# Attention, then two gated MLPs, on one core: PSUM as a ring of four slots, V's products in two bursts per head pair, softmax sums in another form

## The chip, the core and the metric

The kernel runs on one core of one Trainium2 chip. The metric is the device time of one execution in microseconds (us), from the runs of one chip; the version before has a median of 628.54 us over 3 runs (628.42 to 628.84).

## The reference, cut to what matters

```python
# batch 2, heads 8, seq 1152, head_dim 64
q_pool = q.reshape(B, H, S // 2, 2, D).mean(axis=3)           # 576 pooled queries a head
scores = scale * np.matmul(q_pool, k.transpose(0, 1, 3, 2))   # 576 x 1152
scores = scores - np.max(scores, axis=-1, keepdims=True)
attn = np.exp(scores)
attn = attn / (np.sum(attn, axis=-1, keepdims=True) + 1e-09)
x = np.matmul(attn, v)                                        # tokens 1152 x 512
h = x @ w_in;   g = h * np.tanh(softplus(h));   x = g @ w_out     # d_ff 2048
h = x @ w_in2;  g = np.where(h > 0, h, np.exp(h) - 1);  out = g @ w_out2
```

All tensors are float32. The weights of both MLPs come as 64-bit numbers and are turned into float32 on the chip.

## The kernel before, in words

The attention stage takes two heads at a time, a *pair*; there are 8 pairs. Scores are computed with the keys on the partitions: 9 key tiles of 128 keys (`kt`), and the 576 queries in two column groups, `c=0` with 256 and `c=1` with 320 columns. Each score tile (`qk`, line 364) is a sum of three products in a split of float32 into a high and a low part (`KH`/`KL`, `QH`/`QL`), and of a fourth one that adds the negative row maximum from `tops` by a product with `unit`. The two heads of a pair lie on the two halves of the partitions, so each product is two instructions on 64 rows that run side by side. ScalarE takes the exponential of the tile (`exp`, L373) into `pt`, for one key tile, or for two of group 0 at once.

Row maxima of the next pair are computed ahead of need (`peak_mm`, L284, L291, L298; `peak` on VectorE, L305 to L310), and are sent through DRAM into `tops` (`top_out`, `top_in`). V's products (`av`, L444) sum `vs` times `pt` over the 9 key tiles; they are plain float32, which the trace shows as two records for each matmul. The softmax sums come in two steps: `add` (L384) adds key tiles elementwise into two buffers, on GpSimd or VectorE as the table `who` says, and `total` (L399) multiplies by ones and so sums over the partitions. `spill`, `sum_out`, `sum_in`, `invert`, `inv_out` and `inv_in` carry the sums through DRAM and bring their reciprocals back as `rb`. `scale` (L461) multiplies V's product by it in PSUM, and `token_high` and `token_low` (L466, L471) write the two parts `XH` and `XL` for the MLPs.

PSUM has 8 banks, `banks`. Six of them are a ring of three slots of two banks, which `take()` gives out in turn to score tiles and maxima. Bank 6+c holds V's product of group c; the softmax sums and the last 128 columns of the maxima of the 64 left-over queries lie in the free columns of banks 6 and 7.

The order of the work is written out by tables. A step is one key tile, 18 steps a pair. `PLAN` (`FIRST` and `LAST` for the first and last pair) says at which step of a pair, or of the next one (steps over 17), an add, a product of V, a total and each link of the chain behind it are issued; `PREP` says the same for loads, splits and maxima of the next pair. Inside a step the lists go in the order pre, peak, the scores and their exponential, late, av, act, dve, rest, pool, sp. Every engine runs its own instructions in that order. The pieces of the first weights (`Weights`, L119 to L145) are converted in between, one per pair.

The MLP stage (`h_mm` L178, `out_mm` L744) follows. It uses the same 8 banks in another way, and starts with tokens of the first four pairs.

Of the kernel before, what the change touches and what calls it, by code (L numbers as in the profile page):

```python
# [22 lines left out]
def tile_pool_attention_mish_elu_mlp(  # L23
# [20 lines left out]
    P = 128  # L44
# [39 lines left out]
    class Weights:  # L84
# [98 lines left out]
    def attention():  # L183
        with ExitStack() as st:
            ap = st.enter_context(tc.tile_pool(name="attn", bufs=2))
            pools["f"] = st.enter_context(tc.tile_pool(name="f1", bufs=1))
            ring = cycle(range(3))
# [27 lines left out]
            raw_k, raw_q, kh, kl, qh, ql, vs = {}, {}, {}, {}, {}, {}, {}  # L215
            hops, tots, rbs, stat, neg, pts, adds, sc, sums_, acc, xs = {}, {}, {}, {}, {}, {}, {}, {}, {}, {}, {}
# [58 lines left out]
            def peak_mm(n, e):  # L275
# [19 lines left out]
                else:  # L295
                    side = banks[:, 6, 512 - P:]
# [3 lines left out]
            def peak(n, e):  # L300
# [5 lines left out]
                elif t > NQ:  # L306
                    nc.vector.tensor_reduce(m[:, :NQ, :, 2].rearrange("p t h -> p h t"), pt.rearrange("p h (t k) -> p h t k", k=P), axis=AX.X, op=ALU.max)
                else:
                    nc.vector.tensor_reduce(m[:, t, 0, 0:2], pt, axis=AX.X, op=ALU.max)
                    nc.vector.tensor_reduce(m[:, t, 0, 2:3], banks[:, 6, 512 - P:], axis=AX.X, op=ALU.max)  # L310
# [43 lines left out]
            def qk(n, c, kt, m, pt=None, part=slice(4)):  # L354
# [3 lines left out]
                terms = [(kh[n], qh[n]), (kl[n], qh[n]), (kh[n], ql[n]), (None, tops[n % 2])]  # L358
                sc[n, c, kt] = pt[:, :, :m * w].rearrange("p h (m w) -> p m h w", m=m)
                for t in range(m):  # L360
                    k0 = (kt + t) * P
                    for i, (x, y) in list(enumerate(terms))[part]:
                        for h in range(2):
                            nc.tensor.matmul(  # L364
                                pt[:, h, t * w:(t + 1) * w], x[half[h], k0:k0 + P] if x is not None else unit[half[h], :],
                                y[half[h], cols], start=(i == 0), stop=(i == len(terms) - 1),
                            )

# [7 lines left out]
            ADDS = {1: (0, 0, 1), 3: (1, 2, 3), 4: (0, None, 4), 5: (1, None, 5), 6: (0, None, 6), 7: (1, None, 7), 8: (0, None, 8)}  # L376

            def add(n, c, kt, eng):
                w = cut[c][1] - cut[c][0]
                if kt == 1:  # L380
                    adds[n, c] = ap.tile([P, 2, 2, 5 * D], F32, tag="add", name="add")
                x, i, j = ADDS[kt]
                d, p = adds[n, c][:, x, :, :w], pts[n, c]
                eng.tensor_tensor(d, d if i is None else p[:, i], p[:, j], op=ALU.add)  # L384

            def total(n, c):
                w = (cut[c][1] - cut[c][0]) // 2
# [69 lines left out]

            def scale(n, c):
                w = cut[c][1] - cut[c][0]
                x = xs[n, c] = acc.pop((n, c))[:, :w]  # L460
# [15 lines left out]
            def at(s, e, f, *args):  # L476
# [18 lines left out]
            PREP[2] = {
                "load_q": [-29, -29],
                "load_k": [-22, -20],
                "load_v": [-5, 2],
                "pool_q": -25,
                "high_q": -20,  # L500
                "high_k": [-21, -19],
                "blk_q": -18,
                "low_q": -12,
                "low_k": [-8, -15],
                "peak": [-30, -28, -26, -21, -15, -13, -8, -4, 0, 2],
                "top": [[3, 3], [0, 4]],
            }
            PLAN = {
                "who": [{1: 0, 3: 0, 4: 0, 5: 0, 6: 0, 7: 0, 8: 1}, {1: 0, 3: 0, 5: 1, 7: 0, 4: 0, 6: 0}],
                "add": [{1: 3, 3: 4, 4: 3, 5: 3, 6: 4, 7: 1, 8: 1}, {1: 1, 3: 1, 4: 4, 5: 3, 6: 3, 7: 2}],  # L510
                "av": [10, 10, 17, 17, 17, 17, 17, 17, 17, 22, 22, 22, 22, 26, 26, 26, 26, 28],
                "total": [13, 21],
                "chain": [[-1, 1, 1, 2, 5, 5, 9, 12, 13, 13], [-1, 1, 1, 3, 5, 6, 11, 13, 14, 17]],
                "two": [0, 2, 4, 7],
                "weight": [3, 6, 7, 10, 15, 16, 17, 5],
            }
            FIRST = {
                "who": [{1: 0, 3: 0, 4: 1, 5: 0, 6: 0, 7: 0, 8: 0}, {1: 0, 3: 1, 5: 1, 7: 0, 4: 0, 6: 0}],
                "add": [{1: 2, 3: 1, 4: 4, 5: 3, 6: 2, 7: 1, 8: 3}, {1: 2, 3: 2, 4: 4, 5: 1, 6: 3, 7: 1}],
                "av": [10, 10, 17, 17, 17, 17, 17, 17, 17, 22, 22, 22, 22, 26, 26, 26, 26, 28],  # L520
                "total": [13, 21],
# [368 lines left out]
```

## Time and profile before

| | |
|---|---|
| median of 3 runs | 628.54 us |
| span of the profiled execution, first to last instruction | 627.9 us |
| the runs' median less that span | 0.6 us |
| TensorE busy | 613.0 us, 98% of the span |
| VectorE, ScalarE, GpSimd busy | 447.2, 333.9, 224.2 us |
| attention stage, until the first matmul of L178 | 222.2 us |
| MLP stage | 405.7 us |

The profile is of one execution. Its span leaves out what lies before the first and after the last instruction. PE is TensorE, DVE VectorE, ACT ScalarE, POOL GpSimd, SP the engine that issues most DMAs. TensorE starts a matmul while the one before is still draining, so the records of neighbours overlap; how long a matmul holds the engine is read from the start of one record to the start of the next.

### The profile page before, as it was taken

To read this page: it belongs to the slowest core of one execution; us is meant where nothing else is said; L and a number is where in the kernel's file an instruction comes from. 1 tells how busy PE (TensorE), PEld (TensorE's weight loads), DVE (VectorE), ACT (ScalarE), POOL (GpSimd) and SP (SyncE) were. 2 spreads that over 40 slices of the span, in tenths; PEclk is the share of its full clock that TensorE was granted. 3 is DMA by queue.
4 is the path that set the end of the run, shared out by engine and by line. 5 is a ranking of instruction groups with operands and counts; after the bars stand their busy time and mean duration, and the time that the engine had idled before them with its cause. 6 is when DMAs were issued, how large, how long until landed. Compare 5 with 4: busy or idle time off the path is not lost.

```text
span 627.9 us, 11285 instructions
## 1 busy us (share of the span) xinstructions
PE 613.0 (98%) x4434; PEld 533.7 (85%) x4434; DVE 447.2 (71%) x694; ACT 333.9 (53%) x652; POOL 224.2 (36%) x210
## 2 busy tenths in 40 slices
PE   4899999999999999999999999999999999999997
PEld 3777677767766699999999999999999999999995
DVE  5897777878785566745647667669879788995453
ACT  3574665655654445443453454456657667664441
POOL 5688787887883212110113333332210101100000
PEclk9999999999999999999999999999999999999999
DMA  4424334253331444214223222322232223300011
GB/s 135 144 60 136 92 91 129 67 141 101 72 90 34 109 113 142 86 50 133 68 68 104 98 68 67 101 68 67 68 101 67 68 68 103 121 12 21 32 50 50
DMA packets 46975, 53.33 MB, mean 85 GB/s; under 512 B 13834, under 2 KB 36426, under 8 KB 46922
## 3 DMA queue, kind: packets, MB, share of 16 engines
q1 hardware_dynamic: 46698, 52.29, 28.4%
q8 instruction: 34, 0.56, 0.4%
q10 hardware_dynamic: 224, 0.33, 0.2%
q14 instruction: 19, 0.16, 0.1%
HBM read 50.14 MB, written 2.47 MB: 84 GB/s over the span
## 4 chain that ended last, share of the span: by engine, by line
PE 92%; DVE 3%; DMA 2%; SPq 1%; issue 1%; ACT 0%; DVEq 0%
PE banks L178 32%; PE banks L744 31%; PE banks L364 12%; PE banks L444 10%; PE banks L284 3%; PE banks L399 2%; DVE stat L305 2%; PE banks L298 1%; DMA rb<-pop 1%; DMA qr<-in_q_dram 1%; PE banks L291 0%; SPq L239 0%; DVE add L384 0%; DMA tot<-hop 0%; DVE part L769 0%
## 5 line engine op out<-in xcount | busy, mean ns | idle before, releaser
L123 POOL TENSOR_SCALAR wf<-wf 128x512 f32<-128x512 f32 x64 | 44.3, 693 | 252.7 <-ACT wf L119 222.2
L178 PE MATMUL banks<-XH,wh 128*128 128x384 f32 x384 | 129.5, 337 | 0.0
L178 PE MATMUL banks<-XL,wh 128*128 128x384 f32 x384 | 129.4, 337 | 0.0
L178 PE MATMUL banks<-XH,wl 128*128 128x384 f32 x384 | 129.4, 337 | 0.0
L373 ACT ACTIVATE pt<-banks 128x640 f32<-128x640 f32 (+2 forms) x113 | 87.3, 784 | 49.2 <-PE banks L364 30.4
L305 DVE TENSOR_REDUCE stat<-banks 128x2 f32<-128x1024 f32 (+1 forms) x68 | 78.4, 1173 | 15.8 <-PE banks L284 15.5
L384 POOL TENSOR_TENSOR add<-add,pt 128x512 f32<-128x512 f32 (+1 forms) x50 | 77.0, 1552 | 12.1 <-DVE add L384 8.9
L444 PE MATMUL banks<-pt,vr 128*64 128x320 f32 (+1 forms) x576 | 76.7, 411 | 0.0
L178 PEld LDWEIGHTS banks<-XH,wh 128*128 128x128 f32 x384 | 72.0, 187 | 2.3 <-issue 0.5
L178 PEld LDWEIGHTS banks<-XL,wh 128*128 128x128 f32 x384 | 72.0, 188 | 1.8
L178 PEld LDWEIGHTS banks<-XH,wl 128*128 128x128 f32 x384 | 72.0, 188 | 0.0
L744 PE MATMUL banks<-gh,wl 128*128 128x384 f32 x192 | 64.5, 336 | 0.0
L744 PE MATMUL banks<-gl,wh 128*128 128x384 f32 x192 | 64.5, 336 | 0.0
L744 PE MATMUL banks<-gh,wh 128*128 128x384 f32 x192 | 64.4, 335 | 0.0
L698 ACT ACTIVATE gh<-banks 128x384 fp32r<-128x384 f32 x48 | 23.7, 494 | 75.9 <-PE banks L178 75.9
L444 PEld LDWEIGHTS banks<-pt,vr 128*64 128x64 f32 x576 | 38.6, 136 | 27.6 <-issue 3.5
L128 DVE TENSOR_SCALAR wf<-wf 128x512 int32<-128x512 int32 x64 | 45.5, 712 | 18.8 <-POOL wf L123 18.8
L744 PE MATMUL banks<-wl,gh 128*128 128x512 f32 x144 | 56.2, 390 | 0.0
L744 PE MATMUL banks<-wh,gl 128*128 128x512 f32 x144 | 56.2, 390 | 0.0
L744 PE MATMUL banks<-wh,gh 128*128 128x512 f32 x144 | 56.2, 390 | 0.0
L701 DVE TENSOR_TENSOR gl<-g,gh 128x384 fp32r<-128x384 f32 x48 | 30.7, 640 | 32.0 <-ACT g L699 32.0
L724 ACT CAST gh<-g 128x384 fp32r<-128x384 f32 x48 | 24.7, 514 | 48.2 <-DVE g L718 47.9
(87 smaller groups left out, 1224.9 us busy)
## 6 DMA issues: line engine op xcount, KB each, us to landing
raw<-in_moe_w_in_dram SPq DMA_DIRECT2D x28, 512.0 KB
raw<-in_moe_w_out_dram SPq DMA_DIRECT2D x28, 512.0 KB
vr<-in_v_dram SPq DMA_DIRECT2D x16, 288.0 KB
qr<-in_q_dram SPq DMA_DIRECT2D x14, 288.0 KB
kr<-in_k_dram SPq DMA_DIRECT2D x7, 384.0 KB
raw<-in_moe_w_in_dram SPq DMA_DIRECT2D x8, 256.0 KB
raw<-in_moe_w_out_dram SPq DMA_DIRECT2D x8, 256.0 KB
out_dram<-part SPq DMA_DIRECT2D x8, 256.0 KB
```

The source lines that it names most:

```text
L123: nc.gpsimd.tensor_scalar(self.f, self.f, HUGE, -HUGE, op0=ALU.min, op1=ALU.max)
L128: nc.vector.tensor_scalar(f, f, 3, None, op0=ALU.logical_shift_left)
L178: nc.tensor.matmul(pt[:, :TB], w[:, kk * P:(kk + 1) * P], x[:, kk, tk], start=(i == 0), stop=(i == len(terms) - 1))
L305: nc.vector.tensor_reduce(m[:, t, :, j], pt[:, :, :kw], axis=AX.X, op=ALU.max)
L364: nc.tensor.matmul(pt[:, h, t * w:(t + 1) * w], x[half[h], k0:k0 + P] if x is not None else unit[half[h], :], y[half[h], cols], start=(i = ...
L373: nc.scalar.activation(pts[n, c][:, kt:kt + m], sc.pop((n, c, kt)), AF.Exp, scale=SCALE)
L384: eng.tensor_tensor(d, d if i is None else p[:, i], p[:, j], op=ALU.add)
L444: nc.tensor.matmul(acc[n, c][half[h], :w], vs[n][:, h, kt, :], pts[n, c][:, kt, h, :], start=(kt == 0), stop=(kt == KT - 1),)
L698: nc.scalar.activation(gh, h, AF.Mish)
L701: nc.vector.tensor_tensor(gl, g, gh, op=ALU.subtract)
L724: nc.scalar.copy(gh, g)
L744: nc.tensor.matmul(pt, l, r, start=(first and i == 0), stop=(final and i == 2))
```

## The change

PSUM becomes a ring of four slots; V's product takes one slot of it (`acc`) in its first bank, and the softmax sums and the side piece of the maxima lie in the second bank of such a slot. `evac` copies V's product to SBUF on ScalarE, and `scale`, `token_high` and `token_low` work on that copy. The 9 products of a group are issued close together, `total` right behind them. The score term of the maxima is one matmul for both key tiles of a two-tile step. The sums of a group are one chain of adds on GpSimd (the key tiles with `who` 0) and one VectorE reduction along the others (`gather`, `who` 2); a key tile in neither goes to `total` directly. In the last pair the reduction takes 8 of 9 and 9 of 9 tiles. The splits of Q and K and the pooling of Q are placed on GpSimd or VectorE by the entry `eng` of `PREP`. All tables have new numbers.

```diff
-            ring = cycle(range(3))
+            ring = cycle(range(4))
@@ peak_mm
-                    side = banks[:, 6, 512 - P:]
+                    side = sides[n] = (hold[-1] if n else take())[:, 1, 512 - P:]
@@ qk
-                terms = [(kh[n], qh[n]), (kl[n], qh[n]), (kh[n], ql[n]), (None, tops[n % 2])]
+                terms = [(kh[n], qh[n]), (kl[n], qh[n]), (kh[n], ql[n])]
...
+                if part.stop == 4:
+                    for h in range(2):
+                        y = tops[n % 2][half[h], cols]
+                        nc.tensor.matmul(
+                            pt[:, h, :m * w], unit[half[h], :], y if m == 1 else y.unsqueeze(1).broadcast_to([D, m, w]),
+                            start=False, stop=True,
+                        )
@@ sums
+            def chains(n, c):
+                who = plans(n)["who"][c]
+                parts = [[k for k in range(KT) if who.get(k, -1) in x] for x in ((0,), (1, 2))]
+                return [x if len(x) > 1 else [] for x in parts]
...
+            def gather(n, c, ks):
+                p = pts[n, c][:, ks[0]:ks[-1] + 1:ks[1] - ks[0]]
+                nc.vector.tensor_reduce(sums_of(n, c)[:, 1], p.rearrange("p k h w -> p h w k"), axis=AX.X, op=ALU.add)
...
             def total(n, c):
                 w = (cut[c][1] - cut[c][0]) // 2
...
+                pt = sums_[n, c] = acc[n, c][:, 1, :w]
+                ch, p, a = chains(n, c), pts[n, c], sums_of(n, c)
+                merged = KT in plans(n)["who"][c]
+                srcs = [p[:, k] for k in range(KT) if k not in ch[0] + ch[1]]
+                srcs += [a[:, x] for x in range(2 - merged) if ch[x]]
@@ av, scale
-                    acc[n, c] = banks[:, 6 + c]
+                    acc[n, c] = take()
+                    hold.append(acc[n, c])
...
+            def evac(n, c):
+                w = cut[c][1] - cut[c][0]
+                outs[n, c] = late.tile([P, w], F32, tag=f"out{c}", name="out")
+                nc.scalar.copy(outs[n, c], acc.pop((n, c))[:, 0, :w])
...
-                x = xs[n, c] = acc.pop((n, c))[:, :w]
+                x = xs[n, c] = outs.pop((n, c))
@@ PLAN (pairs 1 to 6)
-                "av": [10, 10, 17, 17, 17, 17, 17, 17, 17, 22, 22, 22, 22, 26, 26, 26, 26, 28],
-                "total": [13, 21],
+                "av": [17, 17, 17, 17, 17, 17, 17, 17, 17, 22, 22, 22, 22, 22, 23, 23, 23, 23],
+                "total": [17, 23],
+                "evac": [17, 23],
@@ LAST
+                "who": [{0: 2, 1: 2, 2: 2, 3: 2, 4: 2, 5: 2, 6: 2, 7: 2, 8: 0}, {0: 2, 1: 2, 2: 2, 3: 2, 4: 2, 5: 2, 6: 2, 7: 2, 8: 2}],
```

TensorE, where one of the middle pairs ends and the next begins, before (`banks<-pt,vr` is V's product, `blk` the left-over queries' maxima, `ones` a softmax sum):

```order
L364 MATMUL banks<-QH,KH 128x320 x2
L364 MATMUL banks<-QH,KL 128x320 x2
L364 MATMUL banks<-QL,KH 128x320 x2
L364 MATMUL banks<-top_83,unit 128x320 x2
L444 MATMUL banks<-pt,vr 64x256 x14
L298 MATMUL banks<-KH,blk_89 128x512 x2
L298 MATMUL banks<-KH,blk_89 128x128
L364 MATMUL banks<-QH,KH 128x256 x2
L364 MATMUL banks<-QH,KL 128x256 x2
```

and now:

```order
L365 MATMUL banks<-QH,KH 128x320 x2
L365 MATMUL banks<-QH,KL 128x320 x2
L365 MATMUL banks<-QL,KH 128x320 x2
L372 MATMUL banks<-top_83,unit 128x320 x2
L285 MATMUL banks<-KH,QH 128x512 x2
L463 MATMUL banks<-pt,vr 64x256 x18
L417 MATMUL banks<-pt,ones 32x128 x4
L417 MATMUL banks<-add,ones 32x128 x8
L285 MATMUL banks<-KH,QH 128x512 x2
L365 MATMUL banks<-QH,KH 128x256 x2
```

All 9 key tiles of V's product of group 0 (18 matmuls) and the softmax sum stand in one block, behind a maximum of 512 columns; the maxima of the left-over queries stand four score products earlier, by themselves.

VectorE in the second half of a middle pair, before (`stat<-banks` is a maximum, `add` a softmax sum):

```order
L249 TENSOR_TENSOR QL<-qr,QH 128x576
L305 TENSOR_REDUCE stat<-banks 128x2
L461 TENSOR_TENSOR banks<-banks,rb 128x256
L471 TENSOR_TENSOR XL<-banks,XH 128x256
L424 RECIPROCAL tot<-tot 128x5
L384 TENSOR_TENSOR add<-add,pt 128x2x256
L307 TENSOR_REDUCE stat<-banks 128x2x4
L319 TENSOR_REDUCE neg<-stat 128x2x2
L259 TENSOR_TENSOR KL<-kr,KH 128x768
L305 TENSOR_REDUCE stat<-banks 128x2 x2
L128 TENSOR_SCALAR wf<-wf 128x512
```

and now:

```order
L401 TENSOR_REDUCE add<-pt 128x2x256
L442 RECIPROCAL tot<-tot 128x5
L306 TENSOR_REDUCE stat<-banks 128x2
L260 TENSOR_TENSOR KL<-kr,KH 128x768
L306 TENSOR_REDUCE stat<-banks 128x2
L485 TENSOR_TENSOR out<-out,rb 128x256
L310 TENSOR_REDUCE stat<-banks 128x2
L311 TENSOR_REDUCE stat<-banks 128x1
L495 TENSOR_TENSOR XL<-out,XH 128x256
L306 TENSOR_REDUCE stat<-banks 128x2
L401 TENSOR_REDUCE add<-pt 128x640
L306 TENSOR_REDUCE stat<-banks 128x2
```

The one add of two tiles has become a reduction `add<-pt`, and the other group's stands at the last row shown; the maxima stand closer together.

TensorE at the end of the last pair, where the MLP stage begins behind it, before:

```order
L364 MATMUL banks<-QL,KH 128x320 x2
L364 MATMUL banks<-top_85,unit 128x320 x2
L444 MATMUL banks<-pt,vr 64x256 x12
L399 MATMUL banks<-pt,ones 32x160 x4
L399 MATMUL banks<-add,ones 32x160 x8
L444 MATMUL banks<-pt,vr 64x320 x18
L178 MATMUL banks<-XH,wh 128x384
```

and now:

```order
L372 MATMUL banks<-top_85,unit 128x320 x2
L463 MATMUL banks<-pt,vr 64x256 x18
L417 MATMUL banks<-pt,ones 32x128 x4
L417 MATMUL banks<-add,ones 32x128 x4
L463 MATMUL banks<-pt,vr 64x320 x14
L417 MATMUL banks<-add,ones 32x160 x4
L463 MATMUL banks<-pt,vr 64x320 x4
```

The last two sums stand inside V's products, the sum of group 1 is one source (4 matmuls) instead of three (12), and it is fed by the VectorE reduction over all 9 key tiles.

## Rows read from the trace of the kernel before

**Rows 1.** The page, parts 1 and 4: busy time by engine; the chain by engine.

```profile
PE 613.0 (98%) x4434; PEld 533.7 (85%) x4434; DVE 447.2 (71%) x694; ACT 333.9 (53%) x652; POOL 224.2 (36%) x210
...
PE 92%; DVE 3%; DMA 2%; SPq 1%; issue 1%; ACT 0%; DVEq 0%
```

**Rows 2.** Busy time by stretch: two whole pairs, the last pair in two pieces.

```profile
core 0: us, PE busy (x) PEld busy (x) DVE busy (x) ACT busy (x) POOL busy (x), PEclk, DMA share, GB/s
...
35.93:61.49 25.56, 25.54 (x286) 18.18 (x284) 21.37 (x28) 14.46 (x24) 20.89 (x16) 1.00 0.37 93
...
163.50:189.07 25.57, 25.55 (x286) 18.11 (x284) 20.65 (x29) 15.41 (x27) 20.66 (x16) 1.00 0.31 76
189.07:212.39 23.32, 23.32 (x267) 16.62 (x265) 12.99 (x24) 12.49 (x22) 8.93 (x7) 1.00 0.31 72
212.39:222.17 9.78, 8.90 (x87) 4.71 (x85) 4.60 (x9) 2.42 (x6) 1.27 (x1) 1.00 0.21 61
```

**Rows 3.** PE in order of time, entering and leaving V's products and a sum.

```profile
118.86 0.48 PE L399 MATMUL banks<-pt,ones 128*32 128x160 f32 x8
119.15 0.73 PE L399 MATMUL banks<-add,ones 128*32 128x160 f32 x16
119.81 0.73 PE L284 MATMUL banks<-KH,QH 64*128 64x512 f32 x4
...
121.09 0.28 PE L364 MATMUL banks<-QL,KH 64*128 64x256 f32 x2
121.21 0.28 PE L364 MATMUL banks<-top,unit 64*128 64x256 f32 x2
121.42 2.37 PE L444 MATMUL banks<-pt,vr 128*64 128x320 f32 x16
...
125.55 0.50 PE L284 MATMUL banks<-KH,QH 64*128 64x512 f32 x2
125.98 2.38 PE L444 MATMUL banks<-pt,vr 128*64 128x320 f32 x16
128.29 0.42 PE L364 MATMUL banks<-QH,KH 64*128 64x320 f32 x2
128.54 0.31 PE L364 MATMUL banks<-QH,KL 64*128 64x320 f32 x2
128.69 0.31 PE L364 MATMUL banks<-QL,KH 64*128 64x320 f32 x2
```

**Rows 4.** PE in order of time: a restart inside the score stream.

```profile
135.26 0.30 PE L364 MATMUL banks<-top,unit 64*128 64x320 f32 x2
135.56 0.41 PE L364 MATMUL banks<-QH,KH 64*128 64x320 f32 x2
```

**Rows 5.** PE in order of time, the end of the attention stage.

```profile
216.49 0.75 PE L399 MATMUL banks<-add,ones 128*32 128x160 f32 x16 [0.88 <-DVE add L384]
...
217.17 5.07 PE L444 MATMUL banks<-pt,vr 128*64 128x320 f32 x36
...
222.17 0.45 PE L178 MATMUL banks<-XH,wh 128*128 128x384 f32 x1
```

**Rows 6.** Groups by shape, 61.49 to 189.07 us: VectorE, columns as in the page's part 5.

```profile
L305 DVE TENSOR_REDUCE stat<-banks 128x2 f32<-128x1024 f32 x41 | 49.6, 1220 | 9.8 <-PE banks L284 9.7
...
L249 DVE TENSOR_TENSOR QL<-qr,QH 128x576 fp32r<-128x576 f32 x5 | 5.4, 1073 | 0.0
...
L384 DVE TENSOR_TENSOR add<-add,pt 128x640 f32<-128x640 f32 x5 | 4.3, 854 | 0.0
...
L384 DVE TENSOR_TENSOR add<-add,pt 128x512 f32<-128x512 f32 x5 | 3.5, 695 | 0.0
```

**Rows 7.** The same stretch: GpSimd.

```profile
L384 POOL TENSOR_TENSOR add<-add,pt 128x640 f32<-128x640 f32 x17 | 30.3, 1789 | 0.7 <-ACT pt L373 0.2
```

**Rows 8.** The same stretch: ScalarE.

```profile
L466 ACT CAST XH<-banks 128x256 fp32r<-128x256 f32 x10 | 3.7, 373 | 6.3 <-DVE banks L461 6.3
...
L410 ACT ACTIVATE sum<-banks 128x160 f32<-128x160 f32 x5 | 1.5, 298 | 0.0
```

More of the change, by code (lines that the diff above doesn't have):

```diff
@@ L500, in attention @@
+                "load_k": [-24, -21],
+                "load_v": [-11, 5],
+                "pool_q": -21,
                 "high_q": -20,
[L501 to L506, printed above, removed]
+                "high_k": [-20, -18],
+                "blk_q": -15,
+                "low_q": -16,
+                "low_k": [-4, -8],
@@ L512, in attention @@
-                "total": [13, 21],
-                "chain": [[-1, 1, 1, 2, 5, 5, 9, 12, 13, 13], [-1, 1, 1, 3, 5, 6, 11, 13, 14, 17]],
-                "two": [0, 2, 4, 7],
-                "weight": [3, 6, 7, 10, 15, 16, 17, 5],
+                "who": [{3: 0, 7: 2, 6: 0, 0: 0, 1: 0, 4: 0, 5: 0, 8: 2}, {6: 2, 1: 0, 2: 0, 5: 0, 0: 0, 3: 0, 8: 2, 7: 0, 4: 0}],
+                "add": [{0: 2, 1: 0, 2: 3, 3: 4, 4: 8, 5: 2, 6: 5, 7: 0, 8: 2, 9: 7}, {0: 0, 1: 3, 2: 2, 3: 3, 4: 5, 5: 4, 6: 11, 7: 1, 8: 0, 9: 0}],
@@ L523, in attention @@
+                "av": [14, 14, 14, 14, 14, 14, 15, 15, 15, 23, 23, 23, 23, 23, 23, 23, 23, 23],
+                "total": [14, 23],
+                "evac": [15, 23],
+                "chain": [[0, 2, 2, 3, 4, 5, 6, 9, 12, 21], [0, 1, 2, 4, 10, 10, 13, 14, 15, 18]],
             }
             LAST = {
-                "who": [{1: 0, 3: 1, 4: 1, 5: 1, 6: 1, 7: 1, 8: 0}, {1: 0, 3: 1, 5: 1, 7: 1, 4: 1, 6: 1}],
-                "add": [{1: 5, 3: 4, 4: 3, 5: 4, 6: 5, 7: 2, 8: 1}, {1: 2, 3: 1, 4: 5, 5: 1, 6: 4, 7: 1}],
@@ new lines, in attention, with plans, on @@
+                "av": [17, 17, 17, 17, 17, 17, 17, 17, 17, 21, 21, 21, 21, 21, 21, 21, 24, 24],
+                "total": [17, 21],
+                "evac": [17, 25],
+                "chain": [[0, 2, 3, 4, 6, 6, 11, 14, 15, 18], [0, 1, 1, 4, 6, 8, 8, 14, 16, 18]],
+                "weight": [2, 4, 6, 8, 19, 20, 28, 5],
+                "early": [8, 12, 22],
+            }
+            def plans(n):
+                return FIRST if n == 0 else LAST if n == n_pairs - 1 else PLAN
+            def on(x, f, n):
+                return (("pool", f, n, nc.gpsimd), ("rest", f, n, nc.vector))[x]
@@ L604, in attention @@
                 peak(0, e)
-            spots = [banks[:, 6:8]]
+            spots = [take()]
             qk(0, 0, 0, 1, spots[0], slice(3))
```

109 lines of the change are left out of this document (54 added, 55 removed).

## Prediction

> **What bounds the kernel now.** I read the page first: TensorE is busy for 613.0 of 627.9 us and makes up 92% of the chain that ended last [rows 1]. So the time is what TensorE's stream takes, and the other engines count only where TensorE waits for them. Then the busy time by stretch [rows 2]: from the first pair's V product at 35.93 us to that of pair 6 at 189.07 us six periods pass, 153.14 us or 25.52 each, and TensorE is busy in practically all of it; VectorE is next, with 20.65 of 25.57 us. The MLP stage (from 222.17 us) has the same code before and after, so I look for changes in the 222 us ahead of it. Third, TensorE in order of time. A busy TensorE isn't one at its peak: each time it goes over to another kind of product it loses something, though no idle time is shown. From start to start a score product of 256 columns (two heads side by side) takes 0.12 us (121.09 to 121.21), but the last one ahead of V's product holds 0.21 [rows 3]. V's product itself: 36 records take 5.00 us (217.17 to 222.17, [rows 5]), 16 take 2.31 (125.98 to 128.29, [rows 3]); the difference gives 0.1345 us a record, so 16 should take 2.15, and 0.16 is fixed. The first score product behind it holds 0.25 instead of 0.15 (128.29, 128.54, 128.69). One excursion to V's product thus costs 0.09 + 0.16 + 0.10 = 0.35 us. A softmax sum: 8 records in 0.29 us (118.86 to 119.15), so 24 in 0.87, and they took 0.95; with the same way in and out that is 0.09 + 0.08 + 0.10 = 0.27.
>
> **The change part by part, for one of the six middle periods.**
>
> *Bursts.* Before, a pair has four excursions to V's product (records in groups of 28, 16, 16 and 12) and two separate sums: 4 x 0.35 + 2 x 0.27 = 1.94 us. Afterwards there are two blocks, each of V's 9 tiles with the sum behind: 2 x (0.09 + 0.16 + 0.08 + 0.10) = 0.86. That gives 1.08 back. Two things go the other way. The left-over queries' maxima, which rode on an excursion, now stand alone among scores: one more way in and out, 0.19. And both blocks now follow a maximum of 512 columns instead of one of four; there the way in is dearer, since such a product holds 0.43 us (125.55 to 125.98) where twice 0.12 would do: 0.19 instead of 0.09, so 0.10 more [rows 3].
>
> *Sources of the sums.* They stay five a pair: group 1 loses one (8 records, 0.29), group 0 gains one (128 columns instead of 160, so 0.23): 0.06 back. The joined score term of the maxima streams the same columns; I take nothing.
>
> *Four slots.* The score stream has restarts: at 135.26 a product holds 0.30 instead of 0.15 because the next one's slot isn't free, and the first in the new slot holds 0.25 as well, to judge by its record of 0.41 against 0.31 [rows 3, 4], so 0.25 us together. I count some three of that kind in a period, about 0.6 us (from that row). A slot now comes round after four takes instead of three; this can give back all 0.6, or cost as much, because V's products no longer stand between the scores and give ScalarE and VectorE time. I take +0.3, halfway to the upper end, since while no V product is held the ring is longer than before.
>
> *The held slot.* V's slot comes free after a copy and the spill of the sum on ScalarE, 0.37 and 0.30 us by the nearest rows [rows 8]. Behind a block stand three other takes (a maximum, scores of two tiles with 6 x 0.12 + 0.24 = 0.96 us, a maximum), some 1.4 us, so the copy is hidden. ScalarE has room: 15.41 of 25.57 us [rows 2]. What is queued behind the copy on ScalarE is the next exponential, whose scores also come after the block.
>
> *The sums' adds.* GpSimd has 11 adds a pair as before, now as one chain a group; the longest, six at 1.79 us or 10.7 [rows 7], has from the second tile of group 1 to the middle of the next pair's group 0, over 15 us: hidden. On VectorE two adds (0.85 + 0.70) go, and two reductions over two tiles come, of 1,024 and 1,280 elements. The trace shows no reduction that steps through SBUF from one key tile to the next. From below: the maxima, 1.22 us for 1,024 elements or 1.19 ns each; from above: GpSimd's add, 1.79 us for 640 or 2.80 ns each. I take 1.19, as the row of the same operation on the same engine: 1.22 + 1.53 us. Pooling Q comes over from GpSimd, 1.07 as the like-sized QL [rows 6]. VectorE then has 20.65 - 1.55 + 2.75 + 1.07 = 22.9 us a period. That fits into 24.4, but with 1.5 us to spare instead of 4.9. Scaling in SBUF instead of PSUM I take as equal; it is off TensorE's path. SP issues the same number of DMAs; the sums' trips through DRAM have a reciprocal on VectorE that waits for them, and what stands behind it are maxima. I price that with the rival below.
>
> A middle period thus gains 1.08 - 0.19 - 0.10 + 0.06 + 0.3 = 1.15, to 24.37 us; six of them 6.9 us.
>
> *The last pair.* From 189.07 us on three excursions and two sums (1.59) become one block (0.53): 1.06 back. In the last piece TensorE idles 0.88 us for an add on VectorE [rows 5], which goes; two sources less in the last sum, 0.58; one more switch to a sum and back, -0.24. Together 2.3 us. What could be late next is the reduction over 9 tiles, 5,760 elements, 6.9 us at 1.19 ns. It can begin 0.7 us after the last score; meanwhile TensorE has 36 records of V at 256 columns (3.9), a sum (0.3) and 28 records (3.8), 8.0 us. It just fits.
>
> *The start, to 35.93 us.* One excursion less and one sum joined, 0.5 us; but VectorE, busy for most of that stretch, gets about 1.7 us more (four adds of 0.85 and the pooling, less the splits of Q and K). Between -1.2 and +0.5; I take 0.
>
> Sum: 627.9 - 6.9 - 2.3 = 618.7 us of span, and 619.3 with the 0.6 us by which the median stands above the span.
>
> **The rivals.**
>
> *VectorE takes over (still faster).* With 22.9 us of work and in-order waits for maxima, DRAM trips and GpSimd, it might keep 2.1 of its 4.9 us of idle time. Then the period is 25.0: 6 x 0.5 = 3.0 us, and 1.5 of the last pair's 2.3: 627.9 - 4.5 + 0.6 = 624.0. For it speaks the closeness, against it that some 9 us of V's blocks a period let VectorE catch up.
>
> *The stepped reduction is slow (slower).* At 2.80 ns an element the two reductions take 6.4 us instead of 2.75, VectorE has 26.6 us a period and sets it: +1.1 x 6 = 6.6. The last reduction takes 16.1 us against 8.0 us of cover: 8.1 less 2.3 is 5.8. Time 627.9 + 6.6 + 5.8 + 0.6 = 640.9. It decides from the point where the two take over 5.3 us, or 2.3 ns an element. Against it: every reduction in the trace runs at 1.19 ns [rows 6], though those read PSUM in a row. The Trainium skill, "SBUF — State Buffer", section "Door 1: The DMA port swizzle", has a rule that speaks for it: SBUF is read in lines of 16 bytes, and each access that goes to a new line pays a penalty; the reduction's steps are 2,048 and 2,560 bytes. No run here shows such a read, and the page gives no size, so by the rule the time lies somewhere on the way to this rival's.
>
> *The ring is blocked by V's slot (slower).* If takes behind a block came round before the copy, each of some 14 blocks would cost 0.37 + 0.30 + 0.25 = 0.9 us: 619.3 + 12.6 = 631.9. It decides where the three takes in between are shorter than 0.7 us; the order makes them 1.4.
>
> **How the numbers follow.** The forecast has 0.64 (616 to 622.5 with the bounds of the restarts and of the start); more than that, with all restarts gone and VectorE at ease, 0.09; VectorE as the bound 0.14; the slow reduction 0.09; the blocked ring 0.04. The likeliest time is 619.3 us. The range of 613 to 627 leaves out the two slower cases and a little below. What differs by over 0.2% counts as faster or slower, about what a measurement of this kernel can tell: faster 0.86, within 0.2% 0.04 (the poor end of the VectorE case), slower 0.10.
>
> **What would show it.** Right: V's product blocks 24.0 to 24.8 us apart, two per pair, hardly any idle time before TensorE's scores; the reductions at 1.2 to 1.6 us; the last sum without a wait; the MLP stage still 405 to 406 us. Wrong: VectorE without gaps and TensorE waiting for `stat` (second case), reductions near 3 us (third), scores behind a block waiting for the copy (fourth), or an MLP stage that is longer because the last pair's tokens come late.

## The result and the profile after

The changed kernel takes 633.63 us (median of 4 runs, 632.53 to 634.46) against 628.48 us for the kernel before on the same chip: ratio 1.008 [1.0066, 1.0095]. It is slower by 0.8%; a run over 1.5% above the fastest of its kernel is left out of this and all later ratios. 619.3 us was forecast, and 633.6 lies outside the range of 613 to 627. The profiled execution has a span of 632.5 us against 627.9, where the forecast's sum was 618.7. That is 13.8 us too much, and the rest of the text asks where they went.

The page of the changed kernel, parts 1 and 4, against [rows 1]:

```profile
PE 606.4 (96%) x4356; PEld 530.9 (84%) x4356; DVE 476.4 (75%) x693; ACT 339.6 (54%) x668; POOL 212.6 (34%) x200
...
PE 75%; DVE 13%; DMA 5%; issue 2%; SPq 2%; ACT 1%; POOL 1%; DVEq 0%; ACTq 0%; POOLq 0%
```

TensorE does have less to do, 6.6 us less. But its share of the chain fell from 92% to 75%, and VectorE and the DMAs hold 18% of it instead of 5%: work that TensorE used to cover is on the path. Busy time by stretch, against [rows 2]: two middle periods from one pair's first block of V's product to the next pair's, the last pair in two pieces, and the MLP stage.

```profile
core 0: us, PE busy (x) PEld busy (x) DVE busy (x) ACT busy (x) POOL busy (x), PEclk, DMA share, GB/s
...
110.72:136.95 26.23, 24.46 (x277) 17.89 (x276) 23.59 (x30) 15.85 (x28) 19.98 (x15) 1.00 0.39 102
136.95:162.97 26.02, 24.47 (x278) 17.89 (x276) 24.03 (x30) 15.80 (x28) 19.77 (x15) 1.00 0.37 101
...
187.84:208.78 20.94, 20.94 (x253) 15.61 (x251) 13.63 (x16) 12.01 (x22) 8.34 (x7) 1.00 0.33 87
208.78:226.43 17.65, 11.69 (x99) 5.84 (x97) 16.17 (x12) 3.25 (x9) 0.00 (x0) 0.83 0.11 33
226.43:632.50 406.07, 401.67 (x2160) 383.72 (x2160) 280.66 (x464) 212.48 (x440) 66.25 (x81) 1.00 0.24 77
```

Two places are wrong. Three of the five middle periods take 26.0 to 26.2 us (the first and the last 25.2 and 24.9) instead of 25.5 before and 24.37 forecast; in the two shown TensorE is idle for 1.6 to 1.8 us, and VectorE is busy for 24 us where it had 20.2 to 21.4. And in the last piece TensorE is busy for 11.7 of 17.65 us, at a granted clock of 0.83 on the mean. The five periods from 59.41 to 187.84 us hold 128.43 us against 5 x 24.37 = 121.85: 6.6 too much.

TensorE in order of time, in a middle pair (against [rows 3]); a bracket is the idle time ahead and what ended it:

```profile
110.72 4.11 PE L463 MATMUL banks<-pt,vr 128*64 128x256 f32 x36
114.76 0.43 PE L417 MATMUL banks<-pt,ones 128*32 128x128 f32 x8
115.00 0.62 PE L417 MATMUL banks<-add,ones 128*32 128x128 f32 x16
...
118.86 0.39 PE L365 MATMUL banks<-QH,KH 64*128 64x256 f32 x2 [0.68 <-DVE stat L306]
...
134.19 0.50 PE L285 MATMUL banks<-KH,QH 64*128 64x512 f32 x2 [1.09 <-DVE stat L306]
```

The burst is there, one entry for all nine key tiles and the sum right behind. The waits are new: a slot isn't free because VectorE hasn't yet reduced the maximum in it. VectorE ahead of the second of them:

```profile
130.15 1.25 DVE L401 TENSOR_REDUCE add<-pt 128x512 f32<-128x1024 f32 x1
132.81 0.19 DVE L442 RECIPROCAL tot<-tot 128x5 f32<-128x5 f32 x1 [1.41 <-DMA tot<-hop]
132.92 1.22 DVE L306 TENSOR_REDUCE stat<-banks 128x2 f32<-128x1024 f32 x1
134.06 1.17 DVE L260 TENSOR_TENSOR KL<-kr,KH 128x768 fp32r<-128x768 f32 x1
...
137.42 2.10 DVE L244 TENSOR_TENSOR qr<-qr 128x576 f32<-128x576 f32 x1
```

The two-tile reduction takes the 1.2 us that it was forecast to take. Behind it VectorE stands 1.41 us for a transfer of the sums, with the maximum queued behind; and the pooling of Q takes 2.10 us where 1.07 was set down. VectorE by shape, 59.41 to 187.84 us (five periods), columns as in the page's part 5, against [rows 6]:

```profile
L244 DVE TENSOR_TENSOR qr<-qr 128x576 f32<-128x576 f32 x4 | 8.4, 2103 | 0.0
...
L260 DVE TENSOR_TENSOR KL<-kr,KH 128x768 fp32r<-128x768 f32 x5 | 6.9, 1380 | 0.0
L495 DVE TENSOR_TENSOR XL<-out,XH 128x64 fp32r<-128x64 f32 x5 | 6.5, 1291 | 0.0
...
L495 DVE TENSOR_TENSOR XL<-out,XH 128x256 fp32r<-128x256 f32 x10 | 6.1, 609 | 0.0
...
L485 DVE TENSOR_TENSOR out<-out,rb 128x256 f32<-128x256 f32 x5 | 4.5, 892 | 0.9 <-DMA rb<-pop 0.9
...
L128 DVE TENSOR_SCALAR wf<-wf 128x512 int32<-128x512 int32 x5 | 2.8, 561 | 0.0
```

The same operations in the kernel before. There the scaling and XL had one input in PSUM; KL's inputs were in SBUF as now, and L128 is a shift of the weights with one input:

```profile
L128 DVE TENSOR_SCALAR wf<-wf 128x512 int32<-128x512 int32 x5 | 7.9, 1581 | 0.0
...
L259 DVE TENSOR_TENSOR KL<-kr,KH 128x768 fp32r<-128x768 f32 x5 | 4.7, 949 | 0.0
...
L471 DVE TENSOR_TENSOR XL<-banks,XH 128x256 fp32r<-128x256 f32 x10 | 4.2, 420 | 2.2 <-ACT XH L466 2.2
L461 DVE TENSOR_TENSOR banks<-banks,rb 128x256 f32<-128x256 f32 x5 | 2.1, 418 | 0.0
...
L471 DVE TENSOR_TENSOR XL<-banks,XH 128x64 fp32r<-128x64 f32 x5 | 1.1, 215 | 0.0
```

A subtraction of 64 columns went from 0.215 to 1.29 us, which is about the time of one GpSimd instruction. The Trainium skill ("SBUF — State Buffer", section "Who interferes with whom") says why that can be: a VectorE instruction with two inputs in SBUF shares a port with GpSimd instructions that read SBUF, and the one that issues second stands until the other is through; with one input in PSUM it doesn't share it. The trace agrees: 1.29 and 0.215 us, GpSimd being busy for some 20 us of a period in both kernels. So does the scaling of 256 columns: 0.89 us on the mean of the middle pairs, and 0.41 in the last piece (211.80, below), where GpSimd is busy for 0.00 us.

The end of the last pair: VectorE, ScalarE and TensorE, against [rows 5].

```profile
203.95 7.54 DVE L401 TENSOR_REDUCE add<-pt 128x512 f32<-128x4096 f32 x1 [5.42 <-ACT pt L382]
...
211.80 0.41 DVE L485 TENSOR_TENSOR out<-out,rb 128x256 f32<-128x256 f32 x1
...
213.28 9.99 DVE L401 TENSOR_REDUCE add<-pt 128x640 f32<-128x5760 f32 x1 [0.18 <-ACT pt L382]
```

```profile
212.25 0.40 ACT L490 CAST XH<-out 128x256 fp32r<-128x256 f32 x1 [2.52 <-DVE out L485]
212.56 0.70 ACT L382 ACTIVATE pt<-banks 128x640 f32<-128x640 f32 x1
```

```profile
223.33 0.76 PE L417 MATMUL banks<-add,ones 128*32 128x160 f32 x8 [5.96 <-DVE add L401]
224.03 2.40 PE L463 MATMUL banks<-pt,vr 128*64 128x320 f32 x8
226.36 0.69 PE L178 MATMUL banks<-XH,wh 128*128 128x384 f32 x1
```

Read from the top. The reduction over 8 key tiles holds VectorE for 7.54 us; the scaling stands behind it; ScalarE's cast waits 2.52 us for that scaling, and the last exponential stands behind the cast in ScalarE's order. So the reduction over 9 key tiles begins at 213.28, 4.5 us after the last scores (V's block begins at 208.78), takes 9.99 us, and TensorE stands for 5.96.

### The profile page after: what moved, and what is told of

It reads as the page before. It is cut to its first block, busy times and chain, and to the rows that moved or that the text cites. A ratio compares the mean times of both kernels' runs of the same rounds, so it can differ in the third digit from the quotient of the medians.

```text
span 632.5 us, 11136 instructions
## 1 busy us (share of the span) xinstructions
PE 606.4 (96%) x4356; PEld 530.9 (84%) x4356; DVE 476.4 (75%) x693; ACT 339.6 (54%) x668; POOL 212.6 (34%) x200
## 4 chain that ended last, share of the span: by engine, by line
PE 75%; DVE 13%; DMA 5%; issue 2%; SPq 2%; ACT 1%; POOL 1%; DVEq 0%; ACTq 0%; POOLq 0%
PE banks L178 32%; PE banks L788 31%; DVE stat L306 5%; PE banks L463 4%; PE banks L365 3%; DMA hop<-sum 3%; DVE add L401 2%; DVE qr L244 1%; PE banks L285 1%; DMA tot<-hop 1%; DMA rb<-pop 1%; PE banks L372 1%; DVE stat L310 1%; PE banks L417 1%; DMA qr<-in_q_dram 1%
## 5 line engine op out<-in xcount | busy, mean ns | idle before, releaser
L123 POOL TENSOR_SCALAR wf<-wf 128x512 f32<-128x512 f32 x64 | 47.3, 739 | 255.6 <-ACT wf L119 210.1
L382 ACT ACTIVATE pt<-banks 128x640 f32<-128x640 f32 (+2 forms) x113 | 82.8, 789 | 26.0 <-PE banks L372 25.7
L397 POOL TENSOR_TENSOR add<-add,pt 128x640 f32<-128x640 f32 (+1 forms) x59 | 88.9, 1507 | 5.8 <-ACT pt L382 2.8
L463 PE MATMUL banks<-pt,vr 128*64 128x320 f32 (+1 forms) x576 | 74.9, 413 | 0.0
L463 PEld LDWEIGHTS banks<-pt,vr 128*64 128x64 f32 x576 | 40.1, 138 | 30.7 <-issue 3.5
L742 ACT ACTIVATE gh<-banks 128x384 fp32r<-128x384 f32 x48 | 23.6, 492 | 76.7 <-PE banks L178 76.7
L128 DVE TENSOR_SCALAR wf<-wf 128x512 int32<-128x512 int32 x64 | 38.9, 608 | 14.3 <-POOL wf L123 14.3
```

Of the source, the lines that this page charges most:

```text
L123: eng.tensor_scalar(self.f, self.f, HUGE, -HUGE, op0=ALU.min, op1=ALU.max)
L128: nc.vector.tensor_scalar(f, f, 3, None, op0=ALU.logical_shift_left)
L382: nc.scalar.activation(pts[n, c][:, kt:kt + m], sc.pop((n, c, kt)), AF.Exp, scale=SCALE)
L463: nc.tensor.matmul(acc[n, c][half[h], 0, :w], vs[n][:, h, kt, :], pts[n, c][:, kt, h, :], start=(kt == 0), stop=(kt == KT - 1),)
L742: nc.scalar.activation(gh, h, AF.Mish)
```

## The experiments

The theory at the start: two costs, the long reductions in the last pair and GpSimd's adds stretching VectorE's two-input instructions. Rivals: the burst itself costs; the pooling of Q on VectorE is the culprit; something waits for the adds.

**VectorE's adds in the last pair** (`last_adds`).

```diff
 LAST = {
-  "who": [{0: 2, ..., 7: 2, 8: 0}, {0: 2, ..., 8: 2}],
-  "add": [{0: 2, 1: 0, ...}, {0: 1, 1: 3, ...}],
+  "who": [{0: 1, ..., 7: 1, 8: 0}, {0: 1, ..., 8: 1}],
+  "add": [{0: 1, ..., 8: 1}, {0: 1, ..., 8: 1}],
```

> The changed kernel with one edit: in the last pair VectorE adds tile by tile (8 and 7 adds) instead of one reduction over 9 and over 8 key tiles. Theory A (the two long reductions, 9.99 and 7.54 us, are what the last sum waited 5.96 us for): the wait falls below 1 us, the adds stand at 0.7 to 0.9 us each, the time falls by 4.5 to 6.5 us, to about 628. Rival (VectorE is late there whatever form the sum has, because of the work queued ahead): a wait of 3 us or more stays and the time falls by under 3 us. The middle periods stay at 26.1 us under both.

Measured: 626.38 us, ratio 0.9964 [0.9949, 0.9978]. TensorE in order of time, at the end of the last pair:

```profile
216.88 0.48 PE L417 MATMUL banks<-add,ones 128*32 128x160 f32 x8
217.28 1.30 PE L463 MATMUL banks<-pt,vr 128*64 128x320 f32 x8
218.51 0.44 PE L178 MATMUL banks<-XH,wh 128*128 128x384 f32 x1
```

No wait, and from the sum to the first matmul of the MLP stage 1.63 us instead of 3.03. In the changed kernel the same eight records of V took 2.40 us instead of 1.30: behind the 6 us of idling the clock was granted at the lower of its two levels, half speed (the third number from the right in this row of the changed kernel; in this run the same piece has 1.00):

```profile
223.33:226.36 3.03, 3.03 (x17) 0.98 (x17) 2.26 (x6) 0.75 (x3) 0.00 (x0) 0.50 0.00 1
```

Of the 38.52 us from 187.84 to the first matmul of the MLP stage at 226.36, 7.4 went (187.41 to 218.51 is 31.10): 5.96 of waiting and 1.40 of clock. The MLP stage, which began at the lower level in the changed kernel, takes 405.7 us instead of 406.1. This is over half the miss, and without it the change is a gain of 0.4%.

**Without GpSimd's adds after the first of each chain** (`short_chain`).

```diff
-for i, j in enumerate(ks[1:]):
+for i, j in enumerate(ks[1:] if x else ks[1:2]):
```

> The changed kernel without GpSimd's adds after the first of each chain (so the softmax sums leave out those key tiles; everything else runs). Theory A (VectorE's tensor-tensor instructions with both inputs in SBUF are held while GpSimd runs): XL of 64 columns falls from 0.98 us to 0.22, scaling of 256 columns from 0.76 to 0.42, pooling of Q from 1.67 to about 1.1; VectorE's busy time falls by 2 us a period or more and the middle periods to 24.2 to 24.8 us; time down by 6 to 9 us. Rival (those instructions are slower because of the layout of their SBUF operands): their durations stay as they are, and so do the periods.

Measured: 629.38 us, ratio 1.0011 [0.9998, 1.0023]; 4.3 us less than the changed kernel, where 6 to 9 were expected. The five periods (59.14 to 182.69 us) hold 123.55 us instead of 128.43; in them, VectorE by shape:

```profile
L495 DVE TENSOR_TENSOR XL<-out,XH 128x64 fp32r<-128x64 f32 x5 | 5.1, 1021 | 0.0
L495 DVE TENSOR_TENSOR XL<-out,XH 128x256 fp32r<-128x256 f32 x10 | 4.9, 490 | 0.0
...
L244 DVE TENSOR_TENSOR qr<-qr 128x576 f32<-128x576 f32 x4 | 3.0, 752 | 0.1
```

The pooling falls from 2.10 to 0.75 us with nothing done to it. So the rival, the layout of the operands, is out for the pooling. The 64-column subtraction stays at 1.02 us, against the expectation; GpSimd still has a split of weights (1.28 us) each period, which may hold it.

**The adds stay, nothing reads their result** (`adds_unread`).

```diff
-srcs += [a[:, x] for x in range(2 - merged) if ch[x]]
+srcs += [p[:, ch[x][0]] if x == 0 else a[:, x] for x in range(2 - merged) if ch[x]]
```

> The changed kernel in which TensorE's sum over the partitions reads key tile 's first exponentials instead of the sum that GpSimd's chain has made: the same matmuls and the same GpSimd adds, but nothing waits for the chain. This leaves most key tiles out of the softmax's denominators. It tells apart two readings of the run without the chain's adds (629.4 against 633.6). Theory A (the adds slow VectorE's two-input instructions down, by being there at the same time): nothing changes, pooling of queries still takes 1.67 us and the time is 632 to 635. Rival C (something waits for the chain's end): the time falls to 629 to 631 with the pooling still at 1.67.

Measured: 633.71 us, ratio 1.0083 [1.0064, 1.0103], the same as the changed kernel; five periods from 59.54 to 186.46 us:

```profile
L244 DVE TENSOR_TENSOR qr<-qr 128x576 f32<-128x576 f32 x4 | 8.4, 2104 | 0.0
```

By the medians nothing waits for the chain (the five periods of the profiled execution are 1.5 us shorter, 126.92 us; the time isn't): it costs by running at the same time. That rival is out.

**Pooling of Q back on GpSimd** (`poolq_gpsimd`).

```diff
-"eng": [1, 1, 1, 0],
+"eng": [0, 1, 1, 0],
```

> The changed kernel with one edit: pooling of Q goes back to GpSimd for the pairs 2 to 7. Theory A (VectorE's work and held instructions set the middle periods): VectorE loses 1.67 us a period, the middle periods fall from 26.1 us to 24.5 to 25.2, the time falls by 4 to 8 us. Rival (the periods are set by the ring of slots and by DRAM trips, whatever VectorE has to do): they stay within 0.3 us of 26.1 and the time within 1.5 us. A third outcome: GpSimd, with 1.4 us more, holds VectorE's other instructions longer, and under half of the gain arrives.

Measured: 635.22 us, ratio 1.0091 [1.0062, 1.0121]: no gain, against theory A. The trace was taken at a mean granted clock of 0.66, so its periods can't be held against the others, and where the 2 us that VectorE is rid of went stays open. The third outcome (GpSimd, which takes them over, holds VectorE's other instructions longer) isn't shown.

**The reciprocal two steps later** (`late_invert`). The idle time ahead of it suggested a third cost.

```diff
 PLAN = {
-  "chain": [[...], [0, 1, 3, 3, 6, 9, 12, 13, 14, 17]],
+  "chain": [[...], [0, 1, 3, 3, 8, 9, 12, 13, 14, 17]],
```

> Of the changed kernel, VectorE's reciprocal of the 640-column half's sums is put two steps later (step 8 after the sums instead of 6) in the six middle pairs; nothing else moves. Theory A (VectorE stands still at the head of its queue: the reciprocal waits 1.3 to 1.5 us for the sums' second transfer, the next maximum comes late by that and TensorE stands 1.1 us at the products behind it, in four or five periods): the wait before the reciprocal goes to under 0.3 us, the waits of TensorE for a maximum fall from 6.1 us to about 2, and the time falls by 3 to 5 us, to 629 to 631. Rival B (VectorE is at its rate, 24 of 26.1 us a period, and what it waits here it would wait elsewhere): the idle time shows up before other VectorE instructions, the periods stay at 26.1 and the time within 1 us of 633.6.

Measured: 635.9 us, ratio 1.0114 [1.0101, 1.0127]: 2.3 us worse than the changed kernel, and neither side expected that. Busy time by stretch, the last three of five periods (columns as above), and VectorE's wait for the broadcasts in all five (us in total, times, longest):

```profile
107.99:131.89 23.90, 23.90 (x277) 17.86 (x275) 22.28 (x28) 15.61 (x28) 20.14 (x15) 1.00 0.40 103
131.89:159.97 28.08, 26.11 (x278) 19.23 (x276) 24.23 (x29) 15.76 (x28) 19.72 (x16) 0.94 0.35 96
159.97:188.10 28.13, 25.24 (x277) 18.08 (x276) 24.94 (x30) 15.71 (x28) 21.28 (x16) 1.00 0.28 73
```

```profile
DVE out L485 <- DMA rb<-pop: 5.7, 4, 2.7
```

For three periods (23.91, 24.53 and 23.90 us) it does what was hoped, TensorE hardly idle; the bursts themselves cost nothing. Then VectorE comes to the scaling before the broadcast of the reciprocals has landed, stands for up to 2.7 us, and two periods take 28.1. All five hold 128.55 us, as many as the 128.43 of the changed kernel: the wait had only moved one transfer on, as the rival said. So the 2.3 us don't lie in these periods; in the profiled execution 0.7 us of them lie in the MLP stage (406.86 us), and the rest isn't found.

**Both edits** (`both_fixed`), the diffs of `last_adds` and `late_invert` together.

> The changed kernel with two edits: the last pair's sums by VectorE adds tile by tile (626.4 measured alone), and the reciprocal of the 640-column half two steps later in the six middle pairs. If the two costs lie one behind the other on TensorE's queue (theory A), the savings add: 626.4 less 3 to 5 = 621.5 to 623.5. If VectorE's rate sets the middle periods (rival B), nothing is added: 626 to 627.

Measured: 627.1 us, ratio 0.9975 [0.9957, 0.9993]: nothing is added.

**The first half's reciprocals sent earlier as well** (`early_bcast`), `both_fixed` and

```diff
-"chain": [[0, 1, 4, 4, 6, 9, 13, 16, 17, 17], ...
+"chain": [[0, 1, 4, 4, 6, 8, 11, 16, 17, 17], ...
```

> The version with VectorE adds in the last pair and the later reciprocal (627.1), and, in the six middle pairs, the first half's reciprocals sent out at step 8 instead of 9 and broadcast at step 11 instead of 13. Theory D (the transfers of the sums take a fixed time, some 13 us from the sums to the broadcast; when the steps get shorter, VectorE reaches the scaling before the broadcast has landed: 4.2 us of waits in three places where the reciprocal's waits were 4.5): the wait of the scaling falls under 1 us in all, most middle periods come to 24.0 to 24.6 us instead of 25.0 to 26.2, and the time is 620 to 624. Rival B (VectorE's rate alone sets the middle periods, 24 us of work with what GpSimd's adds stretch): VectorE's idle time moves on and the time stays at 626 to 628.

Measured: 629.61 us, ratio 1.0017 [1.0005, 1.003]. Theory D fell: VectorE's wait for broadcasts is down to 1.0 us, but 2.4 us come back at the reciprocal, and the periods take 25.2 to 27.8 us. In all three orders tried on the full VectorE it met one transfer or another too early.

**All three** (`three_fixed`): `last_adds`, `late_invert` and `short_chain` together.

> The changed kernel with all three costs taken away at once: VectorE adds in the last pair, the later reciprocal, and GpSimd's adds after the first of each chain left out (so key tiles are missing from the denominators, and the time is no candidate). If the three causes are the whole miss, what is left is the prediction's own sum: 618 to 621, with middle periods of 24.0 to 24.4 us and no wait of TensorE for VectorE above 0.5 us in them. If a fourth cause is in it, the time stays at 623 or more and TensorE's waits of the middle periods name it.

Measured: 619.26 us, ratio 0.9849 [0.9836, 0.9862], span 617.3. Two of its periods:

```profile
59.01:82.91 23.90, 23.90 (x277) 17.88 (x275) 21.18 (x27) 15.35 (x27) 5.88 (x5) 1.00 0.42 104
82.91:106.81 23.90, 23.90 (x278) 17.91 (x276) 22.24 (x29) 15.74 (x28) 5.88 (x5) 1.00 0.40 109
```

This is the forecast's own time. The other three periods take 24.59, 25.13 and 23.89 us, so the expected 24.0 to 24.4 holds only on the mean (24.3). VectorE still waits 4.5 us for broadcasts in five periods, but with 21 to 22 us of work a period it mostly catches up: TensorE's waits come to 1.0 us.

**Without VectorE's two-tile reductions** (`no_gather`): `last_adds`, and the two key tiles go to TensorE's sum directly. Theory E: VectorE lacks slack, whoever fills it.

```diff
 PLAN = {
-  "who": [{3: 0, 7: 2, 6: 0, 0: 0, 1: 0, 4: 0, 5: 0, 8: 2}, {6: 2, 1: 0, 2: 0, 5: 0, 0: 0, 3: 0, 8: 2, 7: 0, 4: 0}],
+  "who": [{3: 0, 6: 0, 0: 0, 1: 0, 4: 0, 5: 0}, {1: 0, 2: 0, 5: 0, 0: 0, 3: 0, 7: 0, 4: 0}],
```

> The changed kernel with VectorE's adds in the last pair (626.4 alone) and, in the six middle pairs, without VectorE's two-tile reductions: TensorE's sum takes those two key tiles as sources of their own, one source more in each half. GpSimd's adds stay, and with them what they stretch. VectorE loses 1.25 + 1.52 = 2.8 us of 24.0 a period, TensorE gains two sources at 0.25 to 0.28 us (from 114.33 to 114.58 and to 115.13 us in the run with VectorE's adds), 0.55 us a period. Theory E (the cause is that VectorE has no slack for the 1.3 to 2.6 us that a late transfer holds it, whoever fills it): the middle periods come to 24.5 to 25.0 instead of 26.1, six times, less 3 for TensorE's sources counted in: 618 to 621. Rival A' (GpSimd's adds must go, since they stretch what the path to the next maximum runs through): the periods stay at 25.8 or more and the time at 625 to 629.

Measured: 623.35 us, ratio 0.9924 [0.99, 0.9947]: better than either kernel; 3 us off `last_adds` where 5 to 8 were expected. The runs spread from 621.27 to 628.08 us (but for one of 2094.83), and the profiled one is the fastest: in it one period still has a wait and 25.64 us, the others 24.4.

**The same with the later reciprocal** (`no_gather_late`).

> The run before, and the reciprocal of the 640-column half two steps later, which alone cost 2 us and beside the missing GpSimd adds gained 3. Theory E: with slack on VectorE a later reciprocal is no harm and takes a 1.3 us wait out of each middle period: the same as without it or up to 2 us less, 616 to 621. If it is worse by 2 us or more, the order of the transfers on the queue matters by itself.

Measured: 621.14 us, ratio 0.9879 [0.9865, 0.9893], the best of all versions that leave nothing out.

```profile
58.85:83.25 24.40, 24.40 (x294) 18.38 (x292) 20.04 (x26) 15.34 (x27) 19.81 (x16) 1.00 0.43 103
...
156.95:181.35 24.40, 24.40 (x293) 18.33 (x292) 21.81 (x29) 15.99 (x29) 19.93 (x15) 1.00 0.33 76
```

GpSimd's adds are all there (19.8 us) and the pooling still takes 1.87 us, yet TensorE waits for nothing (the third period takes 24.92 us, the others 24.4). So the adds need not go: VectorE's sum of work and waits must stay clear of the period, and the edit that cost 2 us on a full VectorE gains 2 on this one. `poolq_gpsimd`, which also takes work off VectorE and gained nothing, isn't explained by this.

**A split sum in the last pair** (`last_split`): GpSimd's chain for the first key tiles, VectorE's reduction for the last three and four.

```diff
 LAST = {
-  "who": [{0: 2, ..., 7: 2, 8: 0}, {0: 2, ..., 8: 2}],
-  "add": [{0: 2, 1: 0, ...}, {0: 1, 1: 3, ...}],
+  "who": [{0: 0, ..., 5: 0, 6: 2, 7: 2, 8: 2}, {0: 0, ..., 4: 0, 5: 2, ..., 8: 2}],
+  "add": [{0: 1, ..., 7: 1, 8: 2}, {0: 1, ..., 8: 1}],
```

> The changed kernel with the last pair's sums split: GpSimd adds the first six and five key tiles in a chain, VectorE reduces the last three tiles of the 512-column half (1536 elements a partition) and the last four of the 640-column half (2560 elements) in one instruction each. It asks at what length the stepped reduction leaves the 1.2 ns an element of two tiles (1254 and 1520 ns) for the 1.74 and 1.84 of nine and eight. If the rate rises with the length of the inner run: about 1.35 to 1.5 ns an element, 2.2 and 3.6 us. If it is a matter of there being two or more: 1.75 to 1.84, 2.8 and 4.6 us. If only the long ones are slow: 1.2, 1.85 and 3.1 us. In each case the 6.0 us wait of the last sum goes and the time is 625 to 628, as with VectorE's adds (626.4).

Measured: 629.94 us, ratio 0.9988 [0.9963, 1.0013], with a wait of 2.1 us left at the last sum, so the time isn't the 625 to 628 that was expected. The two reductions, and the scaling between them:

```profile
204.35 1.93 DVE L401 TENSOR_REDUCE add<-pt 128x512 f32<-128x1536 f32 x1 [3.95 <-ACT pt L382]
...
210.02 1.77 DVE L485 TENSOR_TENSOR out<-out,rb 128x256 f32<-128x256 f32 x1
...
215.11 4.58 DVE L401 TENSOR_REDUCE add<-pt 128x640 f32<-128x2560 f32 x1
```

None of the three readings fits: three tiles go at 1.26 ns an element, four at 1.79. The three are of 512 columns and the four of 640, so tile count and width aren't told apart; at 512 columns the step lies between three and eight tiles, at 640 between two and four. The scaling, at 0.41 us in the changed kernel's last pair, takes 1.77 here, where GpSimd's chain runs beside it (208.26 to 213.20).

**The bursts in the kernel before** (`before_bursts`): its three slots, V's products and sums as late as in the changed kernel.

```diff
 PLAN = {
-  "av": [10, 10, 17, 17, 17, 17, 17, 17, 17, 22, 22, 22, 22, 26, 26, 26, 26, 28],
-  "total": [13, 21],
+  "av": [17] * 9 + [22] * 5 + [23] * 4,
+  "total": [18, 24],
```

with the steps behind the second half's sum moved to suit, and in the last pair the products of the first half at step 17 as well.

> The kernel before with one edit: V's products of a pair issued in two blocks (steps 17, and 22 and 23), with the sum behind each, and the chains behind the sums moved with them; V's product stays in its own two banks, scaling stays in PSUM, the ring has three slots, the adds are as before. Theory A (the blocks do save TensorE about 0.8 to 1.1 us a middle period, and the loss in the changed kernel comes from what else it does on VectorE): periods of 24.5 to 24.9 us instead of 25.5, time 621 to 625. Rival (with V's products in blocks the scores stand closer together, and VectorE and ScalarE can't keep up whatever the sums' form): periods of 25.3 us or more, time 627 to 631.

Measured: 657.49 us, ratio 1.0452 [1.0432, 1.0473]. One period, and TensorE's waits between 60 and 212 us:

```profile
71.23:101.75 30.52, 26.26 (x285) 18.22 (x283) 20.98 (x29) 14.92 (x27) 20.78 (x15) 1.00 0.34 87
```

```profile
PE banks L284 <- DVE stat L305: 8.7, 12, 1.0
PE banks L364 <- ACT pt L373: 5.9, 9, 1.1
```

The five periods from 60.79 us hold 150.51 us instead of 127.58, 4.6 us worse a period and far beyond both expectations. TensorE waits for slots whose maxima or exponentials aren't done; the likely reason is that V's products no longer stand between the scores while these are worked off. With three slots and these tables bursts don't pay. Other tables for three slots, and four slots with the old order, were not tried.

## Why the prediction was wrong

*Bursts and four slots: right, and sized too small.* Where nothing holds TensorE a period takes 23.90 us (`late_invert`, `three_fixed`), so 1.6 were gained on it and not 1.15. In such a period (`late_invert`, from 107.99) the score products hold an even 0.12 or 0.15 us from start to start, but for those next to another kind of product: the restarts, 0.6 us by the prediction's count, are gone whole where the sum had half of it. That is 0.3 of the 0.5 us; the rest the runs don't tell apart.

*The two-tile reductions: right.* 1.25 and 1.52 us for 1.22 and 1.53. (The second steps over key tiles 6 and 8, so by 5,120 bytes, not the 2,560 of the prediction; it made no difference.) The chain on GpSimd is hidden, as said: nothing waits for it.

*"Scaling in SBUF instead of PSUM I take as equal; it is off TensorE's path", and pooling at 1.07: the step that failed in the middle periods.* VectorE isn't off the path when its slack is 1.5 us. Per period, from the groups above: low parts of the output (6.5 + 6.1 - 1.1 - 4.2) / 5 = +1.5 us, scaling +0.5, KL +0.4, pooling 8.4 / 5 = 1.7 instead of 1.07. Some of it comes back elsewhere: the shift of the weights, 1.58 us before, takes 0.56, and QL 0.75 instead of 1.07. VectorE ends at 23.6 to 24.2 us a period instead of 22.9. In the period from 110.72 it adds 1.41 us of waiting ahead of the reciprocal, 0.6 for TensorE and 0.5 for a broadcast to 23.6 us of work, and that makes 26.1 of its 26.23. No run left the scaling in PSUM with the rest changed, so what this term alone cost isn't measured; `short_chain` has what GpSimd's adds cost by running beside VectorE, 4.3 us. The rival "VectorE takes over" was this mechanism, put at 25.0 us a period; its argument against itself, that V's blocks let VectorE catch up, didn't hold. The mean of the five measured periods is 25.7.

*The last pair: "6.9 us at 1.19 ns ... It just fits" failed twice.* The rate: 9,994 ns for 5,760 elements is 1.74 ns. And the start: the reduction over 8 tiles had no price in the sum; its 7.54 us hold the scaling, with it a cast on ScalarE, and with that the last exponential. Together 7.4 us, clock included, and 0.4 more in the MLP stage. The "slow reduction" rival spoke of 2.8 ns everywhere; it was right in kind about the long ones alone, at 1.74 and 1.84 ns. The Trainium skill ("SBUF — State Buffer", section "Door 1: The DMA port swizzle") says that an access which crosses to a new 16-byte line pays a penalty. The trace agrees for the long reductions only. All these reductions step by 2,048 bytes or more; at two and three tiles the runs show no price (1.19 to 1.26 ns), from four on one of half as much again (1.74 to 1.84).

*The MLP stage: right to 0.4 us*, 406.1 us against 405.7; its start at the lower clock makes the difference, since `last_adds` has 405.7.

The sum: 13.8 us of miss are 6.6 in five middle periods, 7.7 in the last pair (38.52 us against 33.10 - 2.3), 0.4 in the MLP stage and -0.9 before 59.41 us (35.93 + 24.37 were forecast). With VectorE's costs out, `three_fixed` gives 619.26 us where 619.3 was forecast. That it comes so close is in part luck: its span, 617.3 us, is 1.4 under the sum's 618.7, the start being 1.3 us shorter and the five periods 0.4, and its last pair takes 0.3 us more. But the terms for TensorE hold on the whole; what was missing is on VectorE.

## What to carry to other kernels

Moving an operand from PSUM to SBUF is no neutral edit for a two-input VectorE instruction while GpSimd reads SBUF: price it at its own time plus up to one GpSimd instruction (here 0.2 to 0.4 us became 1.2 to 1.8), and ask where it comes to stand beside one. When a change shortens the bounding engine's period, price the next engine's load together with its waits for transfers (here 1.4 us at a reciprocal, up to 2.7 at a broadcast). The same later reciprocal gained 2.2 us where VectorE had 3 to 4 us to spare, and went with a loss of 2.3 where it had none. And price every instruction that comes new, the first long reduction as well as the last, with what is queued behind it on other engines.

## What the runs showed of the hardware

A VectorE reduction with a step between elements takes 1.19 to 1.26 ns an element over two or three inner elements (1.25, 1.52 and 1.93 us for 1,024, 1,280 and 1,536) and 1.74 to 1.84 over four, eight or nine (4.58, 7.54 and 9.99 us for 2,560, 4,096 and 5,760). A VectorE product of two SBUF tensors of 256 columns takes 0.41 us with GpSimd idle and 1.77 beside its adds. TensorE idle for 5.96 us came back at the lower of its two clock levels (1.2 instead of 2.4 GHz; granted 0.50 from 223.33 to 226.36): eight records took 2.40 instead of 1.30 us. A sum over partitions by TensorE costs only about 0.25 us per key tile (114.76 to 115.00), where a VectorE reduction for two takes 1.25 to 1.52.
